# Two thirds of a gated layer's first products rewritten as seven half-size products, with the float64 weights converted earlier and parked in DRAM

## The chip, the core and the metric

The kernel runs on one core of a Trainium2 chip. Its engines work side by side, each through its own list of instructions in order: TensorE (PE, matrix products; PEld is its weight loader), VectorE (DVE), ScalarE (ACT), GpSimd (POOL) and SyncE (SP, which here only issues DMAs). The metric is the device time of one execution in microseconds; less is better.

## The reference

Three layers in a row, on 1152 tokens of width 512. Only the shapes and the last two layers matter for the change.

```python
attn = ...                      # windowed attention, 2 x 8 heads, 576 tokens, 64 wide
x = attn as (1152, 512)
for e in range(4):              # mixture: 4 experts, 512 -> 1024 -> 512
    h = np.maximum(x @ w1[e], 0.0)
    out += p[:, e:e+1] * (h @ w2[e])
# gated layer, 512 -> 1536 -> 512; its weights arrive as float64
xn = x / rms * rms_g
g = xn @ w_gate
silu = g * (1.0 / (1.0 + np.exp(-g)))
val = xn @ w_val
return (silu * val) @ w_out
```

## The kernel before

All matrix products are made of three float32r products (high x high, high x low, low x high), so every operand is split into a rounded high part (a copy on ACT) and the rest (a subtraction on DVE). `parts_of` is that pair of instructions.

**Mixture.** Each expert is cut into two halves of 512 hidden columns, which makes eight units. Unit 0 is plain. Units 1 to 7 compute `x @ w1` by `products` (L732): seven products of half-size blocks in place of eight, for one of two blocks of hidden columns and one of two groups of 576 tokens. One call issues seven runs of six matmuls of 128x128 by 128x288. ACT copies the first run out of PSUM, DVE forms five sums from the others (L522), and `relu` (L811) writes `h`. The weight sums that the scheme needs come from `load_unit` (L614), the token sums from `token_sums` (L577). After four such calls come nine output tiles, `out_plain` (L845): twelve matmuls of 128x512 each, whose result DVE adds into `y` (`mix`, L874). One unit is 168 + 108 matmuls.

**Gated layer.** Three thirds of 512 hidden columns, u = 0, 1, 2. In each, `gated` (L1028) is called for four blocks of 128 columns and three groups of 384 tokens: twelve matmuls 128x384 for the gate, Silu on ACT, twelve for the value, a multiplication on DVE. So a third is 288 such matmuls, and then nine output tiles as in the mixture, summed into `acc`.

The gated layer's weights come as float64. `converted` (L668) takes a 512 KB piece to float32: one ACT instruction (L680) and three on DVE (L683, L686, L689, integer shifts and masks). There are 36 pieces: 24 of gate and value (`load_chunk`, L695) and 12 of the output matrix (`load_out`, L705). Before, each is loaded, converted and split within the gated layer or just ahead of it (the last stretch of unit 7).

**What sets the order.** A planner (`Plan`, L49) emits the program. TensorE's matmuls are emitted in program order. Work with a due time (`pl.later`: loads, splits, conversions) goes into the gaps of ACT, DVE and the SP queue that the planner's own cost table leaves. The order on each engine is then fixed: an engine waits for the instruction at its head. All DMAs of this part go through SP's one queue. Buffers are rings (`RINGS`, L34): `raw` for loaded weights, `wb` and `wa` for split weights, `s` for converted pieces, `t` for token sums, `oa` for the split `h`.

Of the kernel before, what the change touches and what calls it, by code (L numbers as in the profile page):

```python
# [32 lines left out]
SIGN = -(1 << 31)  # L33
RINGS = {"raw": 2, "wa": 8, "wb": 7, "oa": 5, "s": 4, "t": 2, "x": 2, "r": 2, "a": 2, "b": 2, "c": 2, "d": 2}  # L34
ROOT_GROUPS = ((0, 1, 2), (3, 4, 5), (6, 7, 8))
# [112 lines left out]
def tile_fused(ctx: ExitStack, tc: tile.TileContext, qS, kS, vS, probs, w1, w2, wgv, wo, g, out):  # L148
# [4 lines left out]
    ypool = ctx.enter_context(tc.tile_pool(name="ypool", bufs=1))  # L153
    wraw = ctx.enter_context(tc.tile_pool(name="wraw", bufs=2))
    wpa = ctx.enter_context(tc.tile_pool(name="wpa", bufs=8))
# [102 lines left out]
    with (  # L258
# [168 lines left out]
        def sums():  # L427

            st = [tpre.tile([P, S], F32, tag="t", name="stage", bufs=RINGS["t"]).rearrange("p (a b) -> p a b", a=2) for _ in range(2)]
            (ah, al), (bh, bl), (ch, cl), (dh, dl) = ([x.bitcast(F32) for x in second(n, 0)] for n in (0, 1, 2, 4))  # L430
# [76 lines left out]
    pl = Plan()  # L507
    rings = {n: [End(0.0) for _ in range(k)] for n, k in RINGS.items()}
    mark = len(tc.nc.cur_bb.bb.instructions)

# [23 lines left out]

    def raw_load(src, due, shape=(2, 512), dtype=F32):
        need, done = take("raw")
        box = []

        def emit(e):
            box.append(wraw.tile([P, *shape], dtype, tag="raw", name="raw"))  # L540
            nc.sync.dma_start(out=box[0], in_=src)

        return box, pl.later("q", 512, [need], emit, due), done

# [11 lines left out]
    class Stage:  # L556
# [6 lines left out]
        def first(self, engines, n, needs, emit, due):  # L563
            def emit_first(e):
                self.tile = (tpre if self.tag == "t" else tmp).tile([P, 512 if self.tag == "s" else S], F32, tag=self.tag, name="stage", bufs=RINGS[self.tag])
                emit(e)

            return pl.later(engines, n, needs, emit_first, due, (rings[self.tag], self.done))
# [39 lines left out]

    def load_w1(u):

        slots = [take("wb") + (late(slot_b),) for _ in range(7)]
        return [lambda due, i=i: load_unit(u, i, slots, due) for i in range(2)]

    def load_unit(u, i, slots, due):  # L614
        box, hr, done = raw_load(w1[u, i], due)
        place = {n: 7 * i + k for k, n in enumerate((2, 0, 1, 4, 6, 3, 5) if i else (0, 1, 3, 5, 2, 4, 6))}

# [31 lines left out]
        ]  # L649
        return ops, [x[1] for x in (slots[:3], slots[3:])[i]]  # L650

    def load_w2(u, due):


        out, last = [], []
        for i in range(2):
            box, hr, done = raw_load(w2[u, :, 2 * i : 2 * i + 2, :], due)
            ends = []
            for j in range(2):
                need, d = take("wa")  # L660
                w = late(slot_a)
                ends.append(parts_of(512, lambda p, w=w: w()[:, p, :], lambda j=j, box=box: box[0][:, j, :], [hr, need], due))
                out.append((w, ends[-1]))
                last.append(d)
            done.of = ends
        return out, last

    def converted(src, needs, due):  # L668

        box, hr, done = raw_load(src, due, (512,), I64)  # L670
        st = Stage()
# [22 lines left out]

    def load_chunk(c, due):  # L695
        slots = [take("wb") for _ in range(2)]
        w = [late(slot_b) for _ in range(2)]
        ends = []
        for j in range(2):
            st, x = converted(wgv[c, :, j, :], [], due)  # L700
            ends.append(parts_of(512, lambda p, j=j: w[j]()[:, p, :], lambda st=st: st.tile, [x, slots[j][0]], due))
            st.done.of = [ends[j]]
        return w, ends, [s[1] for s in slots]

    def load_out(u, due):  # L705

        out, last = [], []
        for k in range(4):
            need, d = take("wa")
            st, x = converted(wo[u, :, k, :], [], due)  # L710
            w = late(slot_a)
            end = parts_of(512, lambda p, w=w: w()[:, p, :], lambda st=st: st.tile, [x, need], due)
            st.done.of = [end]
            out.append((w, end))
            last.append(d)
        return out, last

# [96 lines left out]

    def hidden_products(unit, right, i, gr):
        if i == 0:
            rewrite(gr)
        products(
            unit[0], right, HT,
            lambda src, k: relu(i, span(gr, 0), src, k),  # L820
            lambda src, k: relu(i, span(gr, 1), src, k),
            lambda src, k: relu(i + 2, slice(gr * S, (gr + 1) * S), src.rearrange("p a b -> p (a b)"), k),
            ((), unit[1] if gr == 1 else ()),
        )
        flush()
# [72 lines left out]
    first = [operand(*second(n, 0), End(0.0)) for n in range(7)]  # L898
    units = [f(20 + 10 * i) for i, f in enumerate(load_w1(1))]
    right = [first, token_sums(1, End(0.0), w1_read, 28)[0]]  # L900
# [11 lines left out]
    w1_read.of = [k]  # L912
    nxt = load_w2(1, pl.t + 29)
    v = [((lambda x=x: x), End(0.0)) for x in v]
# [9 lines left out]
    squares, weighted, normal, ready = {}, {}, {}, {}  # L924
    chunks, outs = {}, {}

# [55 lines left out]
    for u in range(1, NU):  # L982
# [3 lines left out]
        for i, gr in ((0, 0), (1, 0), (0, 1), (1, 1)):  # L986
            hidden_products(now_units[i], right[gr], i, gr)
            if (i, gr) == (0, 1) and u + 1 < NU:
                more = load_w1(u + 1)
                units.append(more[0](pl.t + 20))  # L990
            elif (i, gr) == (0, 1):
                for c in range(2):
                    chunks[c] = load_chunk(c, pl.t + 28 + 11.5 * c)
            if (i, gr) == (1, 0):
                for t in range(3):
                    parts[t] = plain_parts(t, pl.t + 6 + 2 * t)
        if u + 1 < NU:
            units.append(more[1](pl.t + 20))
            nxt = load_w2(u + 1, pl.t + 30)
        else:  # L1000
# [4 lines left out]
            pl.later("a", 1600, [], lambda e: nc.scalar.activation(out=rstd, in_=ident[:, :NTT], func=AF.Sqrt), pl.t)  # L1005
            chunks[2] = load_chunk(2, start + 10)

# [14 lines left out]
    UNIT = 66.7  # L1022
    for n in range(3, 12):
        chunks[n] = load_chunk(n, start + UNIT * (n // 4) + 11.5 * (n % 4))
        if n % 4 == 3:
            outs[n // 4] = load_out(n // 4, start + UNIT * (n // 4) + 60)

    def gated(w, ends, c, tok, between=lambda: None):  # L1028
# [4 lines left out]
        needs = ends + [ready[t] for t in range(tok.start // P, (tok.stop + P - 1) // P)]  # L1033
        pg, ng, dg = any_bank()
        k = gemm(pg[:, :T], [ng] + needs, lambda k: plain(w, 0, k), tok)
# [4 lines left out]
        k = gemm(pv[:, :T], [nv] + needs, lambda k: plain(w, 1, k), tok)  # L1040
        j = pl.now("d", T, [j, k] + [x for g in grs for x in was_reading[g]], lambda e: nc.vector.tensor_tensor(
# [6 lines left out]

    order = [(c, i) for c in range(2) for i in range(3)] + [(c, i) for i in range(3) for c in (2, 3)]
    for u in range(NV):  # L1050
        parts = {}
        rewrite(0)
        rewrite(1)
        for c, i in order:
            w, ends, read = chunks[4 * u + c]
            tok = slice(3 * i * P, (3 * i + 3) * P)
            if u == 0 and c == 0:
                k = gated(w, ends, c, tok, lambda: transposes(*((3, 4, 5), (6, 7, 8), ())[i]))
            else:
                k = gated(w, ends, c, tok)  # L1060
            if c == 3 and i < 2:
                for t in range(3 * i, 3 * i + 3 - i):
                    parts[t] = plain_parts(t, pl.t + 4 + 2 * (t - 3 * i))
            if i == 2:
                for e in read:
                    e.of = [k]
        right_o, o_read = outs.pop(u)

        def put(t, c, src, needs, u=u):
            dst = acc[:, t, c]  # L1070
            if src.ndim == 3:
                dst = dst.rearrange("p (a b) -> p a b", a=2)
            if u == 0:
# [53 lines left out]
```

## Time and profile before

| what | value |
|---|---|
| median of 3 runs | 686.96 us (686.86 to 686.96) |
| profiled execution, its own time | 687.18 us |
| its span, first to last instruction | 685.4 us |
| PE busy, share of the span | 674.2 us, 98% |
| DVE busy | 443.4 us, 65% |
| ACT busy | 293.1 us, 43% |
| granted TensorE clock | 1.000 of full speed |

The profiled execution is 0.22 us above the median, and 1.78 us of its time lie outside the span. Busy times are sums over the span and say nothing of which engine waits for which; that is read from the chain of waits and from stretches of time.

### The profile page before, as it was taken

What the parts mean: (1) busy time and instruction counts of PE and PEld (TensorE: products, weight loads), DVE (VectorE), ACT (ScalarE), POOL (GpSimd) and SP (SyncE); (2) the same over time, 40 slices, a digit from 0 to 9 for tenths busy, and PEclk for the clock granted to TensorE, in tenths of its full rate; (3) what the DMA queues carried; (4) which work ended last, traced back from release to release, by engine and by line L of the source; (5) the groups of instructions that cost most, each with busy time, mean ns of one, the idle gap of its engine ahead of it and who ended that gap; (6) DMA issues with size and microseconds to landing.
All of it is one profiled execution on the core that took longest, in us unless ns stands there. A gap on an engine that the chain in (4) does not pass through costs nothing.

```text
span 685.4 us, 10489 instructions
## 1 busy us (share of the span) xinstructions
PE 674.2 (98%) x4072; PEld 595.7 (87%) x4072; DVE 443.4 (65%) x946; ACT 293.1 (43%) x666; POOL 54.2 (8%) x108
## 2 busy tenths in 40 slices
PE   8999999999999999999999999999999999999997
PEld 4566788988988989989889889879998999899986
DVE  6677468686585684783865856887786765831223
ACT  6876425452451442633524514755456534301210
POOL 7863410000000000000000000000000000000000
PEclk9999999999999999999999999999999999999999
DMA  8450001203002012021030020104443431200012
GB/s 265 171 166 2 1 0 32 93 15 109 2 32 93 1 44 80 1 93 32 15 110 1 32 92 17 62 1 142 135 144 133 153 133 53 92 1 1 1 46 93
DMA packets 16161, 46.04 MB, mean 67 GB/s; under 512 B 1776, under 2 KB 4080, under 8 KB 16112
## 3 DMA queue, kind: packets, MB, share of 16 engines
q1 hardware_dynamic: 16112, 45.38, 20.1%
q8 instruction: 32, 0.52, 0.3%
q14 instruction: 17, 0.14, 0.1%
HBM read 43.01 MB, written 2.36 MB: 66 GB/s over the span
## 4 chain that ended last, share of the span: by engine, by line
PE 94%; DVE 4%; ACT 1%; issue 0%; POOL 0%; POOLq 0%; DVEq 0%
PE ps_b L854 12%; PE ps_d L854 10%; PE ps_a L854 9%; PE ps_c L854 8%; PE ps_c L750 7%; PE ps_d L750 7%; PE ps_b L208 6%; PE ps_c L208 6%; PE ps_d L208 5%; PE ps_a L208 5%; PE ps_a L750 5%; PE ps_b L750 4%; PE s L333 3%; PE pst L379 3%; PE po L385 2%; PE psa L208 2%
## 5 line engine op out<-in xcount | busy, mean ns | idle before, releaser
L854 PE MATMUL ps_b<-wa,op 128*128 128x512 f32 x348 | 82.4, 390 | 0.0
L854 PEld LDWEIGHTS ps_b<-wa,op 128*128 128x128 f32 x348 | 64.8, 188 | 13.3
L526 ACT ACTIVATE op<-h 128x512 fp32r<-128x512 f32 x95 | 56.6, 622 | 36.0 <-PE ps_d L854 12.2
L854 PE MATMUL ps_d<-wa,op 128*128 128x512 f32 x288 | 67.8, 390 | 0.0
L519 DVE TENSOR_TENSOR op<-h,op 128x512 fp32r<-128x512 f32 x95 | 63.1, 684 | 7.2 <-ACT op L526 6.8
L854 PEld LDWEIGHTS ps_d<-wa,op 128*128 128x128 f32 x288 | 54.0, 188 | 11.1
L854 PE MATMUL ps_a<-wa,op 128*128 128x512 f32 x264 | 61.8, 389 | 0.0
L854 PEld LDWEIGHTS ps_a<-wa,op 128*128 128x128 f32 x264 | 49.5, 188 | 10.2
L854 PE MATMUL ps_c<-wa,op 128*128 128x512 f32 x240 | 56.2, 389 | 0.0
L854 PEld LDWEIGHTS ps_c<-wa,op 128*128 128x128 f32 x240 | 45.0, 188 | 9.4
L208 PE MATMUL ps_b<-xh,wb 128*128 128x384 f32 x160 | 42.4, 335 | 0.0
L526 ACT ACTIVATE wb<-raw 128x512 fp32r<-128x512 f32 (+1 forms) x63 | 30.5, 526 | 21.8 <-DVE raw L519 21.8
L811 ACT ACTIVATE h<-r 128x576 f32<-128x576 f32 x28 | 19.2, 686 | 47.3 <-DVE r L522 47.3
L208 PE MATMUL ps_a<-xh,wb 128*128 128x384 f32 x144 | 38.4, 336 | 0.7 <-ACT xh L526 0.7
L208 PE MATMUL ps_c<-xh,wb 128*128 128x384 f32 x144 | 38.0, 334 | 0.0
L519 DVE TENSOR_TENSOR wb<-raw,wb 128x512 fp32r<-128x512 f32 (+1 forms) x63 | 34.1, 566 | 1.4 <-ACT wb L526 0.8
L208 PE MATMUL ps_d<-xh,wb 128*128 128x384 f32 x128 | 33.9, 334 | 0.0
L680 ACT ACTIVATE stage<-raw 128x512 f32<-128x512 f32 x36 | 23.9, 667 | 22.1 <-DMA raw<-in_wo 11.6
L208 PEld LDWEIGHTS ps_b<-xh,wb 128*128 128x128 f32 x160 | 29.1, 188 | 0.1
L526 ACT ACTIVATE wa<-raw 128x512 fp32r<-128x512 f32 x28 | 16.1, 621 | 28.2 <-DMA raw<-in_w 28.2
L208 PE MATMUL ps_b<-xl,wb 128*128 128x384 f32 x80 | 26.8, 336 | 0.3 <-DVE xl L519 0.3
L750 PE MATMUL ps_c<-xh,wb 128*128 128x288 f32 x112 | 27.0, 297 | 0.0
(224 smaller groups left out, 1490.8 us busy)
## 6 DMA issues: line engine op xcount, KB each, us to landing
raw<-in_w SPq DMA_DIRECT2D x32, 512.0 KB, 3.7
raw<-in_wgv SPq DMA_DIRECT2D x24, 512.0 KB, 3.7
raw<-in_wo SPq DMA_DIRECT2D x12, 512.0 KB, 3.5
kt<-in_kS SPq DMA_DIRECT2D x8, 288.0 KB, 3.3
qt<-in_qS SPq DMA_DIRECT2D x8, 288.0 KB, 3.5
out_y<-acc SPq DMA_DIRECT2D x9, 256.0 KB, 2.0
vt<-in_vS SPq DMA_DIRECT2D x4, 512.0 KB, 4.9
vt<-in_vS SPq DMA_DIRECT2D x4, 64.0 KB, 4.6
```

The source lines that it names most:

```text
L208: nc.tensor.matmul(ps, lhsT=a, rhs=x[:, k, tok], start=(n == 0), stop=(n == 3 * KC - 1))
L333: nc.tensor.matmul(sps[t][o : o + D, :], lhsT=qt[rows, t * D : (t + 1) * D], rhs=kt[rows, k0 : (t + 1) * D], start=True, stop=True,)
L379: nc.tensor.transpose(pst[:nk, j, :], tt[:, 2 * kb + j, c0 : c0 + nk], ident)
L385: nc.tensor.matmul(out, lhsT=vt[:nk, kb, v], rhs=rhs, start=start, stop=stop, skip_group_check=True,)
L519: EN[e].tensor_tensor(out=out, in0=a, in1=b, op=ALU.subtract)
L526: nc.scalar.activation(out=out, in_=a, func=AF.Copy)
L680: j = st.first("a", 512, [hr] + needs, lambda e: nc.scalar.activation(out=st.tile, in_=words(1, F32), func=AF.Copy, scale=2.0**-112,), due)
L750: nc.tensor.matmul(ps, lhsT=s[:, k, :], rhs=t(k), start=start and m == 0, stop=m == 5, skip_group_check=True,)
L811: return wrote(gr, pl.now("a", tok.stop - tok.start, needs + was_reading[gr], lambda e: nc.scalar.activation(out=h[:, c, tok], in_=src, fu ...
L854: nc.tensor.matmul(ps, lhsT=a(s)[:, k, :], rhs=w[k][0]()[:, i, :], start=(n == 0), stop=(n == 11))
```

## The change

The first third of the gated layer stays as it was, with its column blocks in another order. In the second and third, gate and value are computed by `products`, with the same code as in the mixture: for each of two column blocks four calls, gate on two token groups, then value on two token groups. `silu` writes the gate's part of `h` on ACT, `times` multiplies the value into it on DVE. The token sums for the normalised tokens are made by `token_sums` during the first third, the weight sums by `load_unit`.

All 36 float64 pieces are now converted during mixture units 1 to 7: `store` loads a piece into a `scratch` tile, converts it, and writes the float32 result (256 KB) to a DRAM tile; 3 pieces in unit 1's first calls, then 6, 6, 6, 5, 5 and 5 from the end of units 1 to 6 on. The gated layer loads its weights from there as float32, two pieces in one 512 KB DMA, and splits them as the mixture splits its own.

```diff
-RINGS = {"raw": 2, "wa": 8, "wb": 7, "oa": 5, "s": 4, "t": 2, "x": 2, ...
+RINGS = {"raw": 2, "wa": 8, "wb": 7, "oa": 4, "s": 2, "t": 3, "x": 2, ...
...
+    def scratch():
+        return tpre.tile([P, 1024], F32, tag="t", name="scratch", bufs=RINGS["t"])
...
+    coming, gates, outs = [], [], []
+    for src, made in ((wgv, gates), (wo, outs)):
+        for n in range(src.shape[0]):
+            made.append((dram.tile([P, 2, 512], F32, name=f"f{len(gates)}_{len(outs)}"), []))
+            coming += [(src[n, :, j, :], made[-1][0][:, j, :], made[-1][1]) for j in range(2)]
...
-        box, hr, done = raw_load(src, due, (512,), I64)
+        box, hr, done = raw_load(src, due, tag="t", buffer=lambda: scratch().bitcast(I64))
...
+    def store(src, dst, start, due):
+        st, j = converted(src, [End(start)], due)
+        st.done.of = [pl.later("q", 512, [j], lambda e: nc.sync.dma_start(out=dst, in_=st.tile), due)]
+        return st.done.of[0]
...
+    def silu(c, tok, src, needs):
+        gr = tok.start // S
+        gate[c, tok.start] = end = pl.now("a", tok.stop - tok.start, needs + was_reading[gr], lambda e: nc.scalar.activation(
+            out=h[:, c, tok], in_=src, func=AF.Silu,
+        ))
+        return end
+    def times(c, tok, src, needs):
+        return wrote(tok.start // S, pl.now("d", tok.stop - tok.start, needs + [gate[c, tok.start]], lambda e: nc.vector.tensor_tensor(
+            out=h[:, c, tok], in0=src, in1=h[:, c, tok], op=ALU.mult,
+        )))
...
+            if (u, i, gr) == (1, 0, 1):
+                store_next(3, pl.t)
...
+        if u + 1 < NU:
+            store_next(6 if u < 4 else 5, pl.t + 24)
...
+        if u == 0:
+            right, parts = plain_unit_0()
+        else:
+            parts = {}
+            for i in range(2):
+                for put in (silu, times):
+                    unit = units.pop(0)
+                    for gr in range(2):
+                        hidden_products(unit, right[gr], i, gr, put)
```

**TensorE, from the last output tile of the first third into the second third.** A row is one instruction by source line, output and inputs (`wb`: split weights, `xh`/`xl`: tokens high and low, `th`/`tl`: token sums). Before:

```order
L854 MATMUL ps_b<-wa,op 128x512 x24
L854 MATMUL ps_d<-wa,op 128x512 x12
L208 MATMUL ps_d<-xh,wb 128x384
L208 MATMUL ps_d<-xl,wb 128x384
L208 MATMUL ps_d<-xh,wb 128x384 x2
```

After:

```order
L901 MATMUL ps_b<-wa,op 128x512 x24
L901 MATMUL ps_d<-wa,op 128x512 x12
L783 MATMUL ps_b<-xh,wb 128x288
L783 MATMUL ps_b<-xl,wb 128x288
L783 MATMUL ps_b<-xh,wb 128x288 x2
L783 MATMUL ps_b<-xl,wb 128x288
L783 MATMUL ps_b<-xh,wb 128x288
L783 MATMUL ps_b<-th_95,wb 128x288
```

Ahead of this place TensorE's list is the same as before, matmul by matmul. From here each third has 336 matmuls of 288 columns in place of 288 of 384.

**VectorE, unit 2 of the mixture, first two of its four calls of `products`.** The rows on `ps_a` to `ps_d` with `x` and `r` are the five sums of a call. Before:

```order
L884 SCALAR_TENSOR_TENSOR y<-ps_b,pn_sb,y 128x512
L522 TENSOR_TENSOR x<-ps_b,x 128x288
L522 TENSOR_TENSOR r<-ps_d,x 128x288
L522 TENSOR_TENSOR r<-ps_d,r 128x288
L522 TENSOR_TENSOR r<-ps_d,x 128x288
L522 TENSOR_TENSOR x<-ps_d,x 128x288
L522 TENSOR_TENSOR x<-ps_a,x 128x288
L522 TENSOR_TENSOR r<-ps_c,x 128x288
L522 TENSOR_TENSOR r<-ps_c,r 128x288
```

After (`L716`, `L719`, `L722` are the three instructions of a conversion):

```order
L534 TENSOR_TENSOR x<-ps_b,x 128x288
L719 SCALAR_TENSOR_TENSOR stage<-scratch,stage 128x512
L534 TENSOR_TENSOR r<-ps_d,x 128x288
L534 TENSOR_TENSOR r<-ps_d,r 128x288
L531 TENSOR_TENSOR wa<-raw,wa 128x512 x2
L534 TENSOR_TENSOR r<-ps_d,x 128x288
L534 TENSOR_TENSOR x<-ps_d,x 128x288
L722 SCALAR_TENSOR_TENSOR stage<-scratch,stage 128x512
L716 TENSOR_SCALAR stage<-stage 128x512
L534 TENSOR_TENSOR x<-ps_a,x 128x288
L534 TENSOR_TENSOR r<-ps_c,x 128x288
L534 TENSOR_TENSOR r<-ps_c,r 128x288
```

Conversions and the splits of `w2` (`wa`) now stand between the sums; in the first call one of them stands between two sums that TensorE waits for.

**SP's queue in the mixture.** Before, all loads of the mixture stand in one run:

```order
L297 DMA qt<-in_qS 128x576
L541 DMA raw<-in_w 128x1024 x26
L541 DMA raw<-in_wgv 128x512 x2
L1003 DMA g_sb<-in_g 128x512
L541 DMA raw<-in_wgv 128x512 x6
```

After, the stretch of one unit (`f` is a tile in DRAM):

```order
L731 DMA f_0_1311<-stage 128x512
L567 DMA scratch<-in_wgv 128x512
L731 DMA f_0_1311<-stage 128x512
L567 DMA scratch<-in_wgv 128x512
L731 DMA f_0_1312<-stage 128x512
L567 DMA scratch<-in_wgv 128x512
L567 DMA raw<-in_w 128x1024 x4
L731 DMA f_0_1312<-stage 128x512
```

The four loads of the next unit's weights stand behind stores, each of which waits for its conversion.

## Rows read from the trace of the kernel before

**Rows 1.** Page, part 1: busy us (share of the span), instructions.
```profile
PE 674.2 (98%) x4072; PEld 595.7 (87%) x4072; DVE 443.4 (65%) x946; ACT 293.1 (43%) x666; POOL 54.2 (8%) x108
```

**Rows 2.** Page, part 4: the chain that ended last, by engine.
```profile
PE 94%; DVE 4%; ACT 1%; issue 0%; POOL 0%; POOLq 0%; DVEq 0%
```

**Rows 3.** Stretches: length, busy us (count) of PE, PEld, DVE, ACT, POOL; clock; DMA share.
```profile
168.95:191.55 22.60, 22.54 (x169) 22.31 (x169) 12.05 (x25) 8.40 (x19) 0.00 (x0) 1.00 0.03 10
191.55:216.10 24.55, 24.55 (x110) 20.29 (x110) 19.00 (x34) 9.80 (x19) 0.00 (x0) 1.00 0.26 83
451.70:508.26 56.56, 55.23 (x322) 53.77 (x321) 45.75 (x85) 29.68 (x53) 0.00 (x0) 1.00 0.33 112
532.79:582.73 49.94, 49.94 (x289) 49.94 (x289) 32.65 (x57) 21.96 (x39) 0.00 (x0) 1.00 0.33 110
607.25:657.20 49.95, 49.95 (x290) 49.95 (x289) 10.61 (x18) 9.14 (x18) 0.00 (x0) 1.00 0.00 1
```

**Rows 4.** Chain in order of time, unit 2 of the mixture: start us, us, what.
```profile
168.98 0.76 DVE y L884
...
174.83 1.58 PE ps_a L750 x12
176.41 1.60 PE ps_c L750 x12
178.01 0.80 PE ps_a L750 x6
178.80 1.60 PE ps_c L750 x12
...
191.55 4.58 PE ps_b L854 x20
```

**Rows 5.** Chain in order of time, gated layer: output tiles, then 384-column matmuls.
```profile
590.93 5.44 PE ps_c L854 x24
...
611.44 4.16 PE ps_c L208 x24
```

**Rows 6.** Chain in order of time, start of the gated layer.
```profile
453.52 0.33 DVE stage L683
...
459.66 0.34 DVE stage L683
...
464.70 0.60 DVE wb L519
```

**Rows 7.** Groups of VectorE and ScalarE instructions by shape: count | busy, mean ns | idle before.
```profile
L686 DVE SCALAR_TENSOR_TENSOR stage<-raw,stage 128x512 int32<-128x512 int32 x36 | 24.7, 689 | 0.8
L689 DVE SCALAR_TENSOR_TENSOR stage<-raw,stage 128x512 int32<-128x512 int32 x36 | 24.6, 687 | 0.5
L683 DVE TENSOR_SCALAR stage<-stage 128x512 int32<-128x512 int32 x36 | 15.1, 421 | 12.7 <-ACT stage L680 12.5
L680 ACT ACTIVATE stage<-raw 128x512 f32<-128x512 f32 x36 | 23.9, 667 | 22.1 <-DMA raw<-in_wo 11.6 <-DMA raw<-in_wgv 9.7 <-DVE wb L519 0.6
L522 DVE TENSOR_TENSOR r<-ps_c,x 128x288 f32<-128x288 f32 x28 | 12.8, 458 | 18.5 <-PE ps_c L750 17.0
L519 DVE TENSOR_TENSOR raw<-raw 128x256 f32<-128x256 f32 x42 | 17.6, 419 | 0.4
```

**Rows 8.** VectorE in order of time, second call of unit 2 [idle before <- releaser].
```profile
177.33 0.46 DVE L522 TENSOR_TENSOR r<-ps_c,x 128x288 f32<-128x288 f32 x1
178.04 0.46 DVE L522 TENSOR_TENSOR r<-ps_c,r 128x288 f32<-128x288 f32 x1 [0.26 <-PE ps_c L750]
```

**Rows 9.** VectorE in order of time, unit 2: the last split of its `w1`.
```profile
207.01 0.69 DVE L519 TENSOR_TENSOR wb<-raw,wb 128x512 fp32r<-128x512 f32 x1
```

**Rows 10.** DMA issues: count, KB each, median us from issue to landing.
```profile
raw<-in_wgv SPq DMA_DIRECT2D x24, 512.0 KB, 3.7
...
out_y<-acc SPq DMA_DIRECT2D x9, 256.0 KB, 2.0
```

**Rows 11.** Waits of SP's queue, largest: us in total, times, longest.
```profile
SPq L541 <- DVE wb L519: 307.2, 14, 58.8
```

More of the change, by code (lines that the diff above doesn't have):

```diff
@@ L427, in sums @@
         def sums():
-            st = [tpre.tile([P, S], F32, tag="t", name="stage", bufs=RINGS["t"]).rearrange("p (a b) -> p a b", a=2) for _ in range(2)]
+            st = [scratch()[:, :S].rearrange("p (a b) -> p a b", a=2) for _ in range(2)]
             (ah, al), (bh, bl), (ch, cl), (dh, dl) = ([x.bitcast(F32) for x in second(n, 0)] for n in (0, 1, 2, 4))
@@ L649, in load_unit, with load_w2 @@
         ]
-        return ops, [x[1] for x in (slots[:3], slots[3:])[i]]
-    def load_w2(u, due):
+        return ops, [x[1] for x in last]
+    def load_w2(srcs, due):
         out, last = [], []
-        for i in range(2):
-            box, hr, done = raw_load(w2[u, :, 2 * i : 2 * i + 2, :], due)
+        for src, there in srcs:
+            box, hr, done = raw_load(src, due, needs=there)
             ends = []
@@ L693, in converted, with store_next, load_plain_unit @@
         return st, j
[L695 to L698, printed above, removed]
-        for j in range(2):
[L700 to L716, printed above, removed]
+    def store(src, dst, start, due):
+        st, j = converted(src, [End(start)], due)
+        st.done.of = [pl.later("q", 512, [j], lambda e: nc.sync.dma_start(out=dst, in_=st.tile), due)]
+        return st.done.of[0]
+    def store_next(n, start):
+        for _ in range(n):
+            if coming:
+                src, dst, ends = coming.pop(0)
+                ends.append(store(src, dst, start, start + 20))
+    def load_plain_unit(src, there, due):
+        box, hr, done = raw_load(src, due, needs=there)
+        out = []
+        for j in range(2):
+            need, d = take("wb")
+            w = late(slot_b)
+            out.append((w, parts_of(512, lambda p, w=w: w()[:, p, :], lambda j=j: box[0][:, j, :], [hr, need], due), d))
+        done.of = [x[1] for x in out]
+        return out
     def bank(tag):
@@ L898, in tile_fused @@
     first = [operand(*second(n, 0), End(0.0)) for n in range(7)]
-    units = [f(20 + 10 * i) for i, f in enumerate(load_w1(1))]
+    units = [f(20 + 10 * i) for i, f in enumerate(load_w1(*W1[1]))]
     right = [first, token_sums(1, End(0.0), w1_read, 28)[0]]
@@ L1021, in tile_fused, with gated @@
     NV = FF2 // 512
[L1022 to L1028, printed above, removed]
+    plain_units.append(load_plain_unit(*gates[3], start + 22))
+    nxt = load_w2(outs[:2], start + 40)
+    pair = load_w1(*gates[4:6])
+    units = [f(start + 42 + 6 * i) for i, f in enumerate(pair)]
+    units.append(load_one(gates[6], start + 70))
+    def gated(w, c, tok, between=lambda: None):
         T = tok.stop - tok.start
@@ L1032, in gated @@
         f = tmp.tile([P, T], F32, tag="r", name="sg", bufs=RINGS["r"])
-        needs = ends + [ready[t] for t in range(tok.start // P, (tok.stop + P - 1) // P)]
+        needs = [ready[t] for t in range(tok.start // P, (tok.stop + P - 1) // P)]
+        rows = [{c // 2: x[0]} for x in w]
         pg, ng, dg = any_bank()
-        k = gemm(pg[:, :T], [ng] + needs, lambda k: plain(w, 0, k), tok)
+        k = gemm(pg[:, :T], [ng, w[0][1]] + needs, lambda k: plain(rows[0], c // 2, k), tok)
         j = pl.now("a", T, [k, n, roots[0]], lambda e: nc.scalar.activation(out=f, in_=pg[:, :T], func=AF.Silu))
@@ L1047, in gated, with plain_unit_0 @@
         return k
-    order = [(c, i) for c in range(2) for i in range(3)] + [(c, i) for i in range(3) for c in (2, 3)]
-    for u in range(NV):
-        parts = {}
+    x_read = [End(), End()]
+    def plain_unit_0():
         rewrite(0)
         rewrite(1)
-        for c, i in order:
-            w, ends, read = chunks[4 * u + c]
+        right, parts = [], {}
+        for n, (c, i) in enumerate([(c, i) for c in (0, 2) for i in range(3)] + [(c, i) for i in range(3) for c in (1, 3)]):
+            w = [plain_units[2 * (c % 2) + j][c // 2] for j in range(2)]
             tok = slice(3 * i * P, (3 * i + 3) * P)
[L1057 to L1060, printed above, removed]
+            k = gated(w, c, tok, lambda: transposes(*((3, 4, 5), (6, 7, 8), ())[i]) if c == 0 else None)
+            if n < 2:
+                whole = End()
+                whole.of = [ready[t] for t in ((0, 1, 2, 3, 4), (4, 5, 6, 7, 8))[n]]
+                right.append(token_sums(n, whole, x_read[n], pl.t + 40)[0])
+            if c == 3 and i == 1:
+                x_read[0].of = [k]
             if c == 3 and i < 2:
```

93 lines of the change are left out of this document (59 added, 34 removed).

## Prediction

> **What bounds the kernel now.** I read the page first: TensorE is busy 98% of the span and VectorE 65% [rows 1]. A share can hide a stage with another limit, so the chain of waits comes next: 94% of what ended last is TensorE [rows 2]. Third, I cut the span into stages [rows 3]. In the gated layer's second and third thirds TensorE has no gap: 288 matmuls fill 49.94 us, 173.4 ns each. A mixture unit's calls of `products` take 22.60 us and its output tiles 24.55 us, again without a gap that matters. Only the first third is different: 56.56 us, though 288 matmuls at 173.4 ns need 49.94; the rest is transposes and, where the chain leaves TensorE, waits for normalised tokens [rows 3, 6]. So time is won by giving TensorE less to do, and lost where VectorE or a transfer makes it wait.
>
> **What the second and third thirds cost after.** Removed are 2 x 288 matmuls of 384 columns: 49.94 + 49.95 = 99.89 us [rows 3]. Added are 16 calls of `products`, 42 matmuls of 288 columns each. The mixture shows the price of these very calls: from the second call of unit 2 at 174.83 to the first output tile at 191.55 three calls take 16.72 us, 5.573 each or 132.7 ns a matmul [rows 4]. Eight calls are 44.59 us, two thirds 89.18. A unit's first call is dearer: it runs from 168.95 [rows 3] to 174.83, 5.88 us, because one of its PSUM banks still holds the last output tile, which VectorE only begins to read at 168.98 [rows 4]. That is 0.31 us, which I add for the third third, where VectorE adds the last tile into `acc` in the same bank. Into the second third I add none: there the last tile sits in `ps_d`, the call begins in `ps_b`, and ScalarE reads the tile while six matmuls run. The gain is 99.89 - 89.18 - 0.31 = **10.4 us**, or 10.1 if both hand-overs cost.
>
> Is a matmul paid by columns? The three widths say so: 132.7 ns for 288, 173.4 for 384 and 226.7 for 512 (5.44 us for 24) [rows 3 to 5], near 0.42 ns a column and 12 ns a piece. PEld counts as busy all through the 384-column stretch, so weight loads could be thought to set the pace; but 288 columns follow the same line, so at this width they do not yet. The Trainium skill's page "TensorE: Matmul & The Clock Gate", section "Back-to-back issue gap", speaks against the change: it gives sustained streams of weight load and matmul as about 81 ns each at 128 columns and 131 at 512, which depends so little on the columns that more and narrower matmuls lose. An estimate from that page, interpolated, is 102 ns at 288 and 114 at 384: 672 x 102 against 576 x 114 ns, 2.9 us slower. The trace does not agree: its 512-column matmuls take 226.7 ns.
>
> **What the conversions cost in the mixture.** A conversion is 0.689 + 0.687 + 0.421 = 1.80 us on VectorE and 0.667 us on ScalarE [rows 7]. Six in a unit are 10.8 us on VectorE. Unit 2 leaves it idle for 22.60 - 12.05 = 10.6 us in the calls and 24.55 - 19.00 = 5.6 us in the output tiles, 16.1 together [rows 3]: they fit, and VectorE goes to nearly nine tenths. ScalarE, busy 18.2 us of 47.15, gets 4.0 more.
>
> Fitting on average is not enough, since VectorE works in order and TensorE waits for two sums in each call. In the second call the sum into `r` from the third run ends at 177.33 + 0.46 = 177.79, and the run that adds into its bank starts at 178.80: 1.0 us to spare. The next ends at 178.50 and is needed after six more matmuls, at 178.80 + 0.80 = 179.60: 1.1 us [rows 4, 8]. One conversion instruction ahead of a sum (0.69 us) is covered, two in a row (1.38) would cost 0.3 to 0.4 us. In the new order the three sums of the second call stand together, and the first call has a single `L719` between two sums that TensorE needs. So the mixture should stay at 47.15 us a unit. The bounds: nothing, or 0.3 us in each of four calls of some six and a half units, 7.8 us. I take 0.1 us a unit, **+0.6**, nearer the lower end because no two stand together there.
>
> The SP queue now issues 36 stores more, and the next unit's four weight loads stand behind stores that wait for conversions. The last split of the next unit's `w1` starts at 207.01 in the trace, 9.1 us before unit 3 begins at 216.10 [rows 3, 9]; in the new list it stands just ahead of the addition of the last output tile, and what it splits is needed by the second call, 5.9 us into the unit, so some 7 us remain. SP's loads have waited for free buffers so far: 307 us over 14 waits [rows 11]. A store is like the output's, 256 KB landing in 2.0 us, a load takes 3.7 [rows 10]. Six conversions in 47.15 us leave each of the two `s` tiles 15.7 us a turn, against 0.667 + 1.80 + 2.0 = 4.5 us without waits [rows 7, 10]. I price this at zero; the rival below says when it is not.
>
> **VectorE in the gated layer.** The second third's list on VectorE has 40 sums and 8 multiplications of 288 columns (0.458), 4 of 576 (at most 0.92), 16 weight sums and 9 splits of 256 (0.419), 21 splits of 512 (0.69) and 9 additions into `acc` (0.76, as `mix`): 22.0 + 3.7 + 10.5 + 14.5 + 6.8 = 57.5 us [rows 4, 7, 9] in 44.6 + 24.5 us, 83%. The tight place is after a value call: its last two sums and three multiplications (2 x 0.458 + 0.92 + 0.46, 2.3 us) stand before the next call's sums. They end 7.87 us after the call's start, the next two sums at 8.79, and TensorE needs the second at 5.57 + 3.97 = 9.54 [rows 4]. 0.75 us to spare, and no split stands between. Cost zero; if a wait of a semaphore or two eats that, 0.1 to 0.3 us in each of 8 calls, 2 us at most.
>
> **The first third.** TensorE's order is unchanged. On the chain at its start stand 0.33 + 0.34 + 0.60 = 1.27 us of conversion and split work that VectorE does ahead of the tokens' low parts [rows 6]. The two conversion pieces are gone after; but the low parts can't start before ScalarE's high parts, so not all of it comes back, and new token sums and splits arrive. So between -1.3 and +0.7 (one split of 0.69 in the wrong place); I take **-0.3**. The stage's load on VectorE stays near its 45.75 us: some 28 token-sum instructions and three weight sets come, the conversions go.
>
> **The sum.** 687.18 - 10.4 + 0.6 - 0.3 = 677.1 for the profiled execution, of which 1.78 us lie outside the span and stay. It was 0.22 above the median, so the median goes to about **677.0**.
>
> **Rivals.**
> *Part given back (12%).* The sums come late in the mixture, VectorE being nine tenths full. For: 5.3 us of idle time are all that is left of a unit. Against: 1.0 us of slack in each call. At 0.15 to 0.4 us in each of some 26 calls plus the gated layer's 2 us: 680 to 685.6.
> *Slower: SP's queue holds back the weights (5%).* Everything goes through one queue in order. If a store at its head waits, the four loads behind it wait too; ScalarE, which splits them, then blocks with the copies that the calls need. It begins to count where the loads run late by more than the 7 us of slack: each of six units then pays the excess, and it decides from 1.7 us each, which eats the 10.3 us of the sum; 2.1 us each ends at 689.5. Late by 9 us is what that takes; six loads at 3.7 us in a row, unhidden, would be 22. Against: the conversions that the stores wait for have 16 us of idle VectorE time for their 10.8.
> *A matmul paid by the piece (1%).* If 288 columns cost as much as 384 there, 96 more at 173.4 ns add 16.6 us: 703.6. Nothing bears it out, since the mixture runs the same calls at 132.7 ns. The rule of the Trainium skill's page "TensorE: Matmul & The Clock Gate" named above points the same way, with 2.9 us.
> *The expected gain all lost but not more (3%)*, 685.6 to 688.3, by the first rival at its strongest. *More than the forecast (1%)*: the first third's waits vanish, 675.7 or less.
>
> **How the numbers follow.** The forecast, 675.8 to 679.9, has 78%. Its own range is the bounds -1.3 in the first third, and +3 of small waits. A measurement of this kernel tells some 0.2% (1.4 us) from no change. Faster by more: 78 + 12 + 1 = 91%. Within: 3%. Slower: 5 + 1 = 6%. The range is 675.8 to 681.5: above lie half of the first rival and all others, some 16%, below 1%.
>
> **What would show it.** Two stretches of eight calls at 44.6 to 44.9 us, with 132.7 ns a matmul; if these are longer without gaps, the price was wrong. Mixture units of 47.15 us with VectorE near 41 us busy; a longer unit with TensorE waiting for `x` or `r` is the first rival, with TensorE or ScalarE waiting for `wb`, `wa` or a DMA the second. A first third of about 56.3 us. I would be wrong above all if VectorE's order let a conversion wait for its loaded piece or its store with the sums queued behind: then each such wait, minus 1.0 us, is TensorE's.

## The result, and the profile after

The changed kernel takes **676.37 us** (median of 4 runs, 676.25 to 676.38), the kernel before 686.96 beside it (686.86 to 687.22): ratio 0.9845, 95% interval 0.9828 to 0.9862, so 10.6 us or 1.5% faster. 677.0 was forecast. The profiled execution takes 676.36 us, its span 674.6, 10.8 less than before.

The page's first part and its chain by engine, of the changed kernel, answer to [rows 1, 2]:

```profile
PE 663.5 (98%) x4168; PEld 585.2 (87%) x4168; DVE 512.8 (76%) x1107; ACT 312.2 (46%) x711; POOL 54.6 (8%) x108
...
PE 96%; DVE 3%; ACT 1%; issue 0%; POOL 0%; POOLq 0%
```

TensorE executes 96 matmuls more and is busy 10.7 us less. VectorE has 161 instructions and 69.4 us more, and its share of the chain falls all the same. Stretches after, columns as in [rows 3]: unit 2's calls and its output tiles, the gated layer's first third without its start, the second third, its output tiles, the last third.

```profile
169.29:191.91 22.62, 22.56 (x169) 22.33 (x169) 18.63 (x37) 10.79 (x23) 0.00 (x0) 1.00 0.56 184
191.91:216.45 24.54, 24.54 (x110) 20.28 (x110) 21.58 (x40) 11.68 (x22) 0.00 (x0) 1.00 0.33 111
453.15:507.81 54.66, 53.69 (x317) 52.95 (x316) 42.52 (x75) 24.59 (x48) 0.00 (x0) 1.00 0.17 59
532.34:576.92 44.58, 44.58 (x337) 44.58 (x337) 33.45 (x73) 19.01 (x42) 0.00 (x0) 1.00 0.14 48
576.92:601.45 24.53, 24.53 (x111) 20.27 (x110) 18.00 (x35) 5.37 (x10) 0.00 (x0) 1.00 0.06 22
601.45:646.29 44.84, 44.84 (x337) 44.61 (x337) 29.88 (x64) 15.06 (x33) 0.00 (x0) 1.00 0.07 25
```

The two last thirds took 49.94 and 49.95 [rows 3]: 5.36 and 5.11 us are gone there, 10.47 of the 10.8. The first third, counted from where the chain's last output tile ends (452.75 before, 453.15 after), goes from 55.51 to 54.66. The mixture's units are as long as they were, 47.16 for 47.15, with VectorE busy 40.2 us for 31.05. The rest is a loss ahead of the mixture: the chain comes to the first call of `products` at 122.18 instead of 121.85 (below).

The DMA issues, as in [rows 10]:

```profile
scratch<-in_wgv SPq DMA_DIRECT2D x24, 512.0 KB, 4.3
f<-stage SPq DMA_DIRECT2D x36, 256.0 KB, 2.5
```

A load of a piece lands in 4.3 us where 3.7 was taken, a store in 2.5 where 2.0 was.

SP's two longest waits, as in [rows 11]:

```profile
SPq L567 <- DVE wb L531: 280.6, 22, 59.0
SPq L731 <- DVE stage L722: 89.7, 29, 6.0
```

Stores do stand in front of loads (29 waits for a conversion, 6.0 us the longest), and still the trace lists no wait of TensorE between 165 and 452 us. (The hand-overs at the start of a unit, some 0.3 us each, are not in that list; the last experiment below removes them.)

### The profile page after: what moved, and what is told of

Its sections match the earlier page's. It is cut to its first block, busy times and chain, and to the rows that moved or that the text cites. A ratio compares the mean times of both kernels' runs of the same rounds, so it can differ in the third digit from the quotient of the medians.

```text
span 674.6 us, 11038 instructions
## 1 busy us (share of the span) xinstructions
PE 663.5 (98%) x4168; PEld 585.2 (87%) x4168; DVE 512.8 (76%) x1107; ACT 312.2 (46%) x711; POOL 54.6 (8%) x108
## 4 chain that ended last, share of the span: by engine, by line
PE 96%; DVE 3%; ACT 1%; issue 0%; POOL 0%; POOLq 0%
PE ps_b L901 13%; PE ps_c L783 10%; PE ps_d L783 10%; PE ps_d L901 9%; PE ps_a L901 8%; PE ps_c L901 8%; PE ps_a L783 8%; PE ps_b L783 7%; PE ps_b L209 3%; PE s L337 3%; PE pst L383 3%; PE po L389 2%; PE ps_a L209 2%; PE ps_c L209 2%; PE psa L209 2%; PE ps_d L209 2%
## 5 line engine op out<-in xcount | busy, mean ns | idle before, releaser
L538 ACT ACTIVATE op<-h 128x512 fp32r<-128x512 f32 x95 | 57.5, 626 | 58.9 <-PE ps_d L901 27.4
L538 ACT ACTIVATE wb<-raw 128x512 fp32r<-128x512 f32 (+1 forms) x98 | 49.9, 537 | 46.0 <-DVE raw L531 45.6
L901 PEld LDWEIGHTS ps_d<-wa,op 128*128 128x128 f32 x276 | 51.7, 188 | 10.7
L531 DVE TENSOR_TENSOR wb<-raw,wb 128x512 fp32r<-128x512 f32 (+1 forms) x98 | 54.6, 575 | 2.3 <-ACT wb L538 1.9
L531 DVE TENSOR_TENSOR wa<-raw,wa 128x512 fp32r<-128x512 f32 (+1 forms) x50 | 32.0, 653 | 14.3 <-ACT wa L538 14.3
L538 ACT ACTIVATE wa<-raw 128x512 fp32r<-128x512 f32 (+1 forms) x50 | 28.4, 598 | 22.1 <-DMA raw<-in_w 19.9
L783 PE MATMUL ps_c<-xh,wb 128*128 128x288 f32 x160 | 38.6, 297 | 0.0
L783 PE MATMUL ps_d<-xh,wb 128*128 128x288 f32 x160 | 38.6, 296 | 0.0
L783 PE MATMUL ps_a<-xh,wb 128*128 128x288 f32 x160 | 38.3, 294 | 0.0
L783 PE MATMUL ps_b<-xh,wb 128*128 128x288 f32 x160 | 38.2, 294 | 0.0
L534 DVE TENSOR_TENSOR r<-ps_c,x 128x288 f32<-128x288 f32 x44 | 20.1, 457 | 16.1 <-PE ps_c L783 13.6
L534 DVE TENSOR_TENSOR r<-ps_d,x 128x288 f32<-128x288 f32 x44 | 20.1, 457 | 10.5 <-PE ps_d L783 8.7
```

The source lines that it names most:

```text
L531: EN[e].tensor_tensor(out=out, in0=a, in1=b, op=ALU.subtract)
L534: EN[e].tensor_tensor(out=out, in0=a, in1=b, op=ALU.add)
L538: nc.scalar.activation(out=out, in_=a, func=AF.Copy)
L783: nc.tensor.matmul(ps, lhsT=s[:, k, :], rhs=t(k), start=start and m == 0, stop=m == 5, skip_group_check=True,)
L901: nc.tensor.matmul(ps, lhsT=a(s)[:, k, :], rhs=w[k][0]()[:, i, :], start=(n == 0), stop=(n == 11))
```

## The experiments

Spans and times of experiments are compared with the changed kernel's 674.6 and 676.37 us; a ratio is to the kernel before, run on the same chip. The kernel before has medians of 686.96 and 687.29 us on the chips used, so 0.3 us between two experiments tell nothing.

### The conversions moved, the products not

The gated layer's three thirds as in the kernel before, with matmuls of 384 columns (`plain_third`), its weights loaded from the DRAM tiles as float32:

```diff
-            right, parts = plain_unit_0()
...
-                        hidden_products(unit, right[gr], i, gr, put)
...
+        plain_units, parts = plain_third(u, plain_units)
```

> Only one part of the change: all 36 conversions in the mixture, weights parked as float32 and reloaded, but gate and value of all three thirds as plain 384-column matmuls. If the gain comes from TensorE's columns (the prediction's step), the second and third thirds take 49.9 us each again and only the first third may keep its gain: 685.5 to 687.0. Rival: taking the conversions out of the gated layer is worth something by itself, because they stood in VectorE's way there: 681 to 684.

687.01 us for 687.29, ratio 0.9997 (0.9987 to 1.0006): no difference, at the upper edge of what was expected. Its first third shows the same 54.66 us as the changed kernel, with VectorE at 24.75 us:

```profile
452.66:507.32 54.66, 53.69 (x317) 52.95 (x316) 24.75 (x45) 20.91 (x40) 0.00 (x0) 1.00 0.21 68
```

So the first third's 0.85 us belong to the moved conversions, and the 10.5 us of the two others to the products alone.

### Matmuls of 288 columns for 384

The kernel before, its plain gated products in four token groups instead of three:

```diff
-            tok = slice(3 * i * P, (3 * i + 3) * P)
+            tok = slice(i * HT, (i + 1) * HT)
```

> The kernel before with its gated layer's plain products in 4 groups of 288 tokens instead of 3 of 384: 384 matmuls of 288 columns in each third for 288 of 384, the same columns in all, nothing else. Theory (TensorE's time goes by columns, 173.4 ns at 384 and 132.7 at 288, so 0.42 ns a column and 12 ns a matmul): 384 x 132.7 = 50.96 us for 288 x 173.4 = 49.94, so 1.0 us a third and 3.1 in all; 690 us, 689 to 692. Rival (by the piece, 173 ns each whatever the width): 96 x 0.173 = 16.6 us a third, 737 us. By the Trainium skill's page on TensorE, the gap in a run goes from 81 ns at 128 columns to 131 at 512, which gives about 102 ns at 288 and 115 at 384, and 384 x 102 for 288 x 115, 6 us a third: 705 us.

689.61 us, ratio 1.0036 (1.0023 to 1.0049), 2.3 us slower. The chain in its second third:

```profile
533.51 1.58 PE ps_d L208 x12
535.08 3.18 PE ps_a L208 x24
...
584.38 2.74 PE ps_d L854 x12
```

24 matmuls take 3.18 us, 132.5 ns each, for 4.16 us at 384 columns [rows 5]. A third of 384 pieces runs from 533.51 to 584.38, 50.87 us for 49.94: 96 pieces more cost 0.93 us. TensorE is paid by columns, with 10 to 12 ns a piece. The Trainium skill's page "TensorE: Matmul & The Clock Gate", section "Back-to-back issue gap", whose figures, interpolated, gave an estimate of 705 us, is not borne out by this stream.

### Conversions left beside the gated products

Twelve conversions stay in the mixture, from the end of its units 5 and 6 on; twelve go to the start of the gated layer and twelve to the end of its first third:

```diff
-            store_next(6 if u < 4 else 5, pl.t + 24)
+            store_next(6 if u >= 5 else 0, pl.t + 24)
...
+    store_next(12, start)
...
+        if u == 0:
+            store_next(12, pl.t)
```

> The changed kernel with 12 of its 36 conversions in the mixture (units 5 and 6), 12 at the start of the gated layer and 12 at the end of its first third, so 24 of them stay beside the gated products and none stands beside the attention. Theory (the move is what makes room for the products by halves): the gated thirds' VectorE has 33.5 and 29.9 us in 44.6 and 44.8 us; 12 conversions of 2.7 us are 32 us more in the first and in the second third, so VectorE has 65 us or more of work there and TensorE waits: the time is 20 to 45 us over the changed kernel's 676.4, so above 690. Rival (the move was not needed, and the products alone would have brought the gain): under 680 us.

721.76 us, ratio 1.0505 (1.0489 to 1.0521): 45 us slower than the changed kernel, just over the range. TensorE's longest wait:

```profile
PE ps_b L783 <- ACT th L538: 29.2, 1, 29.2
```

The chain where the second third should begin:

```profile
544.58 5.25 DMA f<-stage
...
549.94 0.67 ACT stage L713
...
551.82 0.70 DVE stage L722
552.53 4.49 DMA f<-stage
```

That stretch, columns as in [rows 3]:

```profile
533.00:564.00 31.00, 3.19 (x17) 2.56 (x15) 23.32 (x39) 10.30 (x18) 0.00 (x0) 0.63 0.69 221
```

With twelve conversions in one go at these two places the gain is lost. That they have to leave the gated layer altogether is not shown: no run spreads them through it beside the new products. And the reason was only half mine. VectorE is idle for 7.7 of these 31 us, and the 2.7 us that I gave a conversion stand in no row: on VectorE it is 1.80 [rows 7]. The chain is one conversion after another, each waiting for an earlier store to give its tile back, while `th`, which TensorE needs, stands behind them on ScalarE: a conversion waiting for its store with other work queued behind, as at the end of the prediction, but on ScalarE in place of VectorE.

### Every store twice

```diff
+        k = pl.later("q", 512, [j], lambda e: nc.sync.dma_start(out=spare, in_=st.tile), due)
-        st.done.of = [pl.later("q", 512, [j], lambda e: nc.sync.dma_start(out=dst, in_=st.tile), due)]
+        st.done.of = [pl.later("q", 512, [k], lambda e: nc.sync.dma_start(out=dst, in_=st.tile), due)]
```

> The changed kernel with every converted piece also written to a spare place in DRAM first: 36 stores of 256 KB more on SP's queue, on the same buffers, nothing else; the outputs are the reference's. Theory (SP's queue has room: no unit of the mixture waited for a load in the changed kernel's trace, and the 36 stores that the change added cost nothing that shows): within 0.5 us of the changed kernel's 676.4 us. Rival (the queue is close to its end, and the weights of the next unit come late as soon as a store is waited for twice): 1 us or more slower, with waits of the splits of weights for a load, and of TensorE for those splits.

678.18 us, ratio 0.9869 (0.9853 to 0.9885), span 1.9 us longer: more than I gave it, and not by the rival's way. 1.6 us of it is one wait at the end of the mixture, for a split of `h`, behind other work of VectorE:

```profile
450.13 0.75 DVE y L933
...
451.27 0.66 DVE xl L532
451.93 0.61 DVE op L532
...
452.58 2.57 PE ps_d L903 x10
```

The changed kernel has no such split among these instructions, and the kernel with late conversions, without a store more, has the same wait (1.58 us at 452.70): it comes of VectorE's order, which the planner set anew. A load came onto the chain once, at 305.70. The call behind it began at 311.77, 0.21 us later than in the changed kernel, but 0.16 of that was there one unit earlier (264.57 for 264.41), without a load on the chain. So the rival's mechanism is seen for some 0.05 us. TensorE's other waits are those of the changed kernel: 36 stores more cost little on the queue, and more by another order on VectorE.

### More work for VectorE

Each conversion's last VectorE instruction is made once more, or, with `range(3)`, three times (the result stays):

```diff
+        for _ in range(1):
+            j = pl.later("d", 512, [j], lambda e: stt(out=bits(), in0=words(1), ...), due)
```

> The change, with each conversion's last VectorE instruction given once more (same result): 36 x 0.69 us more on VectorE, about 4 us in a unit with six conversions. A unit has 40.2 us of VectorE work in 47.15 after the change. If idle VectorE time is what hides the conversions, 44 us still fit and the time stays within 0.7 us of 676.4, units at 47.15 us. Rival (sums come late once VectorE is nine tenths full): 0.15 us or more in each of some 26 calls, 680 or more.

> As the run with one more, but three more: 36 x 2.07 us, about 12 us in a unit with six conversions, 51 to 52.6 us in 47.15. If VectorE's room is the cover, it is gone here: what does not fit is done later, some 20 us too much by the end of the mixture, and the time rises by 5 to 25 us. Rival: something else than VectorE's idle time hides the work (a queue that is never full): within 1 us of 676.4.

699.28 us (ratio 1.0181, 1.0159 to 1.0203) and 760.97 (1.1079, 1.1061 to 1.1098): 23 and 85 us slower than the changed kernel. Both theories were far too low, and the thought behind them, that 5 us of VectorE's idle time in a unit are room, fell. The first one's rival said 680 or more, and that held, but TensorE does not wait for the sums that it named. What TensorE waits for with one more:

```profile
PE ps_d L905 <- DVE op L531: 7.1, 2, 4.1
PE ps_b L905 <- DVE op L531: 3.7, 1, 3.7
PE ps_c L905 <- DVE op L531: 2.9, 2, 1.9
```

`op` is the low part of `h` for an output tile. VectorE in order of time at the first of these:

```profile
201.45 0.75 DVE L935 SCALAR_TENSOR_TENSOR y<-ps_d,pn_sb,y 128x512 f32<-128x512 f32 x1 [0.18 <-PE ps_d L905]
202.11 0.68 DVE L726 SCALAR_TENSOR_TENSOR stage<-scratch,stage 128x512 int32<-128x512 int32 x1
202.71 0.42 DVE L716 TENSOR_SCALAR stage<-stage 128x512 int32<-128x512 int32 x1
203.17 0.69 DVE L719 SCALAR_TENSOR_TENSOR stage<-scratch,stage 128x512 int32<-128x512 int32 x1
203.89 0.69 DVE L722 SCALAR_TENSOR_TENSOR stage<-scratch,stage 128x512 int32<-128x512 int32 x1
204.62 0.69 DVE L726 SCALAR_TENSOR_TENSOR stage<-scratch,stage 128x512 int32<-128x512 int32 x1
205.23 1.88 DVE L531 TENSOR_TENSOR op<-h,op 128x512 fp32r<-128x512 f32 x3
```

The stretch up to the wait's end, and the next:

```profile
193.20:205.90 12.70, 8.66 (x38) 6.79 (x37) 11.49 (x20) 6.32 (x12) 0.00 (x0) 0.97 0.57 170
205.90:210.70 4.80, 4.74 (x11) 3.81 (x12) 2.55 (x7) 0.01 (x1) 0.00 (x0) 0.50 0.59 205
```

Five conversion instructions stand ahead of the split, TensorE waits 4.10 us, and then ten matmuls take 4.64 us at a granted clock of 0.50, half of the full speed. In the whole run TensorE is busy 673.6 us for 663.5 with the same matmuls: of the 25.4 us of span, 13.7 are these waits and 10.1 are matmuls that took longer, most of them in stretches at a lower clock.

Is it the place in the list or the amount? Four kernels asked that: a smaller amount, 128 or 256 of the 512 columns; and, with one more in full, a later due time for the conversions, or an earlier one for the splits in `plain_parts`.

```diff
+        j = pl.later("d", 128, [j], lambda e: stt(out=bits()[:, :128], ...), due)
...
-                ends.append(store(src, dst, start, start + 20))
+                ends.append(store(src, dst, start, start + 60))
...
-        end = parts_of(512, w, lambda: src, [na] + ..., due)
+        end = parts_of(512, w, lambda: src, [na] + ..., due - 150)
```

> The changed kernel with the last VectorE instruction of each conversion made once more on 128 of its 512 columns, some 0.29 us (estimate from 0.42 at 256 and 0.69 at 512 columns), so 1.7 us more for VectorE in a unit of the mixture: 41.9 of 47.16; the outputs are the reference's. Theory (room was there up to some 42 us a unit; in the run with a later due time the first three units went without a wait at 40.5 to 41.4 us): 676.2 to 678 us. Rival (the list leaves no room at all, any instruction more goes ahead of a split that TensorE waits for): 680 us or more, with waits of TensorE for op of 2 us or more.

> The same on 256 of the 512 columns: 0.42 us a conversion, 2.5 us a unit, VectorE at 42.7 of 47.16 us. Theory (between the quarter and the whole instruction, which cost 23 us): the first waits of TensorE for op appear, 677 to 690 us. Rival (the cost is one of the place in the list, not of the amount): as the whole instruction, 695 us or more.

> The changed kernel with the last VectorE instruction of each conversion made once more (as in the run with one more, 699.3 us), and with the time by which the conversions are due set 40 us later in the list, so that the list sets other work on VectorE ahead of them; the outputs are the reference's. Theory formed from that run (VectorE has room for 4 us more in a unit, and the 23 us came of the place that the list gave the additional instructions, ahead of the splits of h in the output tiles): 676 to 680 us, and no wait of TensorE for the splits of h that is over 0.5 us in the mixture. Rival (VectorE has no room for 4 us a unit, wherever they stand): 690 us or more.

> The changed kernel with the last VectorE instruction of each conversion made once more in full (that run: 699.3 us, 23 over the changed kernel), and with the splits of h for the output tiles due so early in the list that they go ahead of the conversions; the outputs are the reference's. Theory (TensorE was held up by the place of a few splits behind conversions in VectorE's order, not by the amount of work, 44.4 us in a unit of 47.16): 677 to 684 us, and no wait of TensorE for op over 1 us in the mixture. Rival (44.4 us in order is too much for a unit wherever the splits stand; something else then comes late): 690 us or more, with waits of TensorE for weights (wb, wa) or for the sums (x, r).

The times, with VectorE's and TensorE's busy time on the page (span and busy times are of the profiled execution, which with 512 columns took 701.81 us, 2.5 over its median):

| added to each conversion | time, us | ratio (95%) | span | VectorE busy | TensorE busy |
|---|---|---|---|---|---|
| nothing | 676.37 | 0.9845 (0.9828 to 0.9862) | 674.6 | 512.8 | 663.5 |
| 128 columns | 680.53 | 0.9903 (0.9888 to 0.9918) | 679.0 | 520.5 | 664.4 |
| 256 columns | 683.28 | 0.9948 (0.9934 to 0.9961) | 681.5 | 524.8 | 664.8 |
| 512 | 699.28 | 1.0181 (1.0159 to 1.0203) | 700.0 | 533.9 | 673.6 |
| 512, conversions due later | 694.51 | 1.0110 (1.0095 to 1.0125) | 692.6 | 536.5 | 670.1 |
| 512, splits first | 687.37 | 1.0002 (0.9993 to 1.0012) | 685.0 | 530.8 | 665.4 |

The quarter cost 4.2 us where I expected under 2, with two waits for `op` of 1.3 and 1.2 us. Its rival named 680 us, which it reached, and waits of 2 us, which it did not. The half cost 6.9, inside its range. The later due time brought back 4.8 us; 676 to 680 was far off, TensorE still waits for `op` up to 3.7 us in the mixture, and the rival's 690 or more held. With the splits first the waits for `op` are gone and 12 of the 23 us come back, but other work is late now:

```profile
PE ps_a L787 <- DVE wb L531: 4.0, 4, 1.1
PE ps_b L787 <- DVE y L935: 2.5, 4, 1.0
```

That misses the theory's 677 to 684, and the rival's 690 too. Both have a part.

The loss is not spread evenly over the units. Three units, each from its first call to the next unit's, columns as in [rows 3]: with 128 columns more, unit 3; with 512, units 1 and 6.

```profile
217.40:266.22 48.82, 47.35 (x276) 42.51 (x277) 42.14 (x85) 22.34 (x45) 0.00 (x0) 1.00 0.47 140
123.00:171.43 48.43, 47.38 (x277) 42.53 (x277) 38.43 (x74) 21.77 (x45) 0.00 (x0) 1.00 0.32 97
377.06:424.25 47.19, 47.05 (x276) 42.58 (x277) 41.09 (x79) 21.45 (x44) 0.00 (x0) 1.00 0.43 128
```

With 128 columns more, units 3 and 4, of six conversions each, take 48.82 and 48.63 us, and the other five are at most 0.1 us longer than in the changed kernel; 1.08 us more are lost in the first third, where no conversion stands. With 512, units 5 and 6, of five conversions, keep 47.24 and 47.19 us, while unit 1, with three conversions and VectorE busy for 38.43 us alone, loses 1.28 us by a wait of 0.99 for `op`. So the amount of work in a unit does not decide by itself. Over the whole span the growth is 57 to 58% of what VectorE is busy more in three kernels (4.4 of 7.7, 6.9 of 12.0, 10.4 of 18.0 us), 76% with the conversions due later (18.0 of 23.7) and 120% with 512 columns (25.4 of 21.1), the lower clock counted; these are sums over units that lost and units that did not, and no price of a microsecond on VectorE. How much of it another order could save stays open.

### The rings alone, and the loss ahead of the mixture

```diff
-RINGS = {..., "oa": 5, "s": 4, "t": 2, ...}
+RINGS = {..., "oa": 4, "s": 4, "t": 3, ...}
```

> The kernel before with two numbers of the change alone: the ring t has 3 buffers for 2, and, for the room in memory, the ring oa 4 for 5. Theory (the changed kernel reaches the first products of unit 0 0.33 us later, 122.15 for 121.82, because a third buffer lets VectorE take the sums of the next group ahead of the last sums that the first group waits for): the first products at 122.1 to 122.2, every stage after it as before, 687.6 us for 687.3. Rival (the 0.33 us come of another part of the change): 121.8, and 687.3 us.

The time, 687.45 for 686.96 (ratio 1.0005, 0.9996 to 1.0014), can't tell 0.3 us, but the trace can. The chain comes to the first call of `products`, with the addition of the output tile ahead of it, at 122.15 in this kernel, 121.85 before, 122.18 after. The chain of the kernel with the rings alone:

```profile
82.27 1.68 DVE xl L433
83.95 1.77 DVE stage L519
...
87.51 1.74 DVE stage L433
...
89.28 0.69 ACT th L437
...
122.15 0.76 DVE y L882
```

The sum of line 519, for the next group, stands ahead of the two of line 433 that the first group waits for. Before, two buffers held the next group's first sum back until 87.06, and this one until 90.93. So the third buffer that the conversions use costs 0.3 us. (The run has the ring `oa` at 4 too, which was not tried by itself; the sum that moved is in the ring `t`.)

### The last output tile in another bank

The changed kernel, with a unit's ninth output tile in PSUM bank `a`, which the next unit's first call needs last:

```diff
-        ps, need, done = any_bank()
+        ps, need, done = bank("a") if t == NTT - 1 else any_bank()
```

> The change, with the ninth output tile of each unit and third in a PSUM bank (ps_a) that the next call of products does not begin with. In the trace TensorE stands at each hand-over until VectorE has read the last tile: 0.26 to 0.31 us in units 1 to 7 and in the last third. If that wait is what makes a unit's first call dearer, eight hand-overs give 2.1 to 2.5 us: 673.9 to 674.3. Rival: the first call then waits for the next thing (ScalarE's copy or another bank) and the gain is under 0.7 us.

673.92 us, ratio 0.9810 (0.9795 to 0.9825), 2.4 faster than the changed kernel and the fastest of all. The hand-over that [rows 4] show is gone; units begin at 168.74 and 215.56, 46.82 us apart for 47.16. Seven units at 0.31 to 0.34 us and the last third at 0.25 make up most of the 2.7 us of span. So each hand-over was a wait for the bank:

```profile
212.84 2.72 PE ps_a L901 x12
215.56 1.58 PE ps_b L783 x12
```

## Why the prediction was right, step by step

**The gated thirds: right, within 0.1 us.** -10.4 was forecast, 10.47 measured: 44.58 and 44.84 us for 44.59 and 44.90. Even the one hand-over stands where it was put. The chain of the changed kernel at the start of the second and of the last third:

```profile
532.34 1.58 PE ps_b L783 x12
...
601.45 1.84 PE ps_b L783 x12
```

0.26 us for 0.31. Payment by columns was shown twice more, by the width alone and by the move alone.

**The mixture: +0.6 forecast, +0.07 in seven units.** Right that it stays, mis-sized within its bounds. What failed is the step's reasoning. "They fit" was taken from 16.1 us of idle time, and 1.0 us of room ahead of the sums into `r` was named as the tight place. The runs with more work put the tight place in the output tiles, at the splits `op`, and show that 7 us idle in a unit are no measure of room: 1.7 us more lengthened two of the three units with six conversions by 1.5 to 1.7 us, and 3.4 us more cost at most 0.1 us in two units with five. The mixture stayed as it was by an order that happened to fit, which no idle sum could tell: on this step the forecast was lucky. The first rival, part of the gain given back, was nearer than the prediction had it, by another wait than the one named.

**The first third: -0.3 forecast, -0.85 measured,** mis-sized, inside its bounds. The chain after leaves TensorE at its start only for 1.3 us of `xh` and `xl` (453.62 to 454.95); not only the two conversion pieces are gone but most of the waits around them. The kernel with the conversions moved alone has the same stretch.

**SP's queue: zero, right.** No load was late in the changed kernel; 36 further stores cost 1.9 us, 1.6 of them by VectorE's order and 0.05 by a late load. **VectorE in the gated layer: zero, right.** 33.45 and 29.88 us in the two stretches, and no gap on TensorE; with its output tiles 51.45 us in the second third for 57.5 worked out. Busy time counts an overlap of two neighbours once; the 107 instructions, added up one by one, are 55.9 us.

**Not foreseen: +0.33 ahead of the mixture,** 0.30 of it by the ring of three buffers, to which the prediction gave no price. For the profiled execution 677.1 was forecast, 0.7 high: 0.5 from the mixture and 0.55 from the first third, less these 0.33; the rest is within 0.1.

## What to carry to other kernels

Where TensorE fills a stretch without a gap, cost a change of its products by columns from the same kernel's own rows; that was good to a tenth of a microsecond here. Idle time on an engine that works in order is not room by itself: ask for each result that the bound engine needs next how many instructions may stand ahead of it, and test the margin by making one of the moved instructions twice. A pool's number of buffers sets an order too, even far from the place for which it was changed.

## What the runs showed of the hardware

A late result can cost more than its wait, since the granted clock fell behind some of the waits: after 4.10 us without work it was 0.50 for the next 4.80 us (1.2 GHz for 2.4), and in the run with late conversions 0.63 in the stretch with a wait of 29.2 us. The length of the wait does not tell it alone. With 512 columns more, a wait of 1.92 us was followed by 4.20 us at 0.59, and ten matmuls took 4.14 us; with 256, the longest wait, 2.05 us, left the clock at 1.00, and ten matmuls took 2.57. What else decides is not shown. The two stretches, in this order:

```profile
221.80:226.00 4.20, 4.14 (x11) 3.31 (x12) 2.75 (x6) 1.23 (x3) 0.00 (x0) 0.59 0.44 118
300.20:305.00 4.80, 4.71 (x21) 3.89 (x22) 4.61 (x11) 1.31 (x3) 0.00 (x0) 1.00 0.65 166
```

VectorE's sums of 576 columns take 0.75 us, and 1.68 to 1.85 while GpSimd works on `op` (81.76 to 88.66 us). From VectorE and GpSimd in order of time, changed kernel, and last the first of these sums in the kernel before, where it fell beside GpSimd's work (81.69 to 88.28):

```profile
80.68 0.75 DVE L531 TENSOR_TENSOR scratch<-xh 128x576 f32<-128x576 f32 x1
83.89 1.85 DVE L531 TENSOR_TENSOR scratch<-scratch,xl 128x576 f32<-128x576 f32 x1
...
81.76 6.90 POOL L180 TENSOR_TENSOR op<-h,op 128x512 fp32r<-128x512 f32 x4 [9.84 <-ACT op L179]
...
87.06 1.85 DVE L519 TENSOR_TENSOR stage<-xh 128x576 f32<-128x576 f32 x1
```

The same sum took 0.75 us in one kernel and 1.85 in the other, and that made an instruction in the wrong place dear ahead of the mixture. The Trainium skill's page "SBUF — State Buffer", section "SBUF: two separate sides", tells of a port pair that VectorE, when an instruction has two inputs in SBUF, shares with GpSimd: the one that has it keeps it for a whole instruction, and the other is blocked. The rows agree in that VectorE's instructions take longer meanwhile, and no run here separates the port from another cause.
